# The head of a decay-attention and two-MLP kernel, put in order by a small list scheduler

## The chip, the cores and the metric

The kernel runs on one core of one Trainium2 chip. The metric is the device time of one execution in microseconds (us), lower is better. The profile is one execution of the same program, recorded by the hardware profiler; its times are counted from the start of its span. Engines: PE is the matrix engine (TensorE), DVE the vector engine, ACT the scalar engine, POOL is GpSimd, SP is the engine that issues most of the transfers.

## What is computed

Cut from the reference: a linear attention with a decay for each head, then two MLPs on its output.

```python
# q, k, v: batch 2, 8 heads, 768 steps, head size 64, float32
for t in range(S):
    state = gamma * state + einsum('bhd,bhe->bhde', k[:, :, t], v[:, :, t])
    y[:, :, t] = scale * einsum('bhd,bhde->bhe', q[:, :, t], state)
x = y.transpose(0, 2, 1, 3).reshape(1536, 512)
h = x @ w_in                                  # 512 -> 2048
g = where(h > 0, h, exp(minimum(h, 0)) - 1)
x = g @ w_out                                 # 2048 -> 512
out = ((x @ w_a) * (x @ w_b)) @ w_out2        # 512 -> 1536 -> 512
```

The weights arrive as 64-bit floats.

## The kernel before

**Attention.** The two batches times four pairs of heads make eight "pairs". A pair's 768 steps are six chunks of 128, worked in two halves of three chunks. Per pair, PE makes the chunk states (10 small matmuls into a bank `yk`, L271) from keys that ACT has scaled (`decay_k`, two instructions, `kd`, L232); DVE copies the first state and carries the decay through the others (`st`, L274 and L276). Per half, PE makes scores (6 matmuls into `sc`, L246), DVE masks them (`a`, L254), PE adds the state part and the score part of the result (10 or 12 matmuls into a bank `yk`, L294 and L300), DVE scales it (`yf`, L308), ACT rounds it to the high part `xh` (L320) and POOL makes the rest `xl` (L321).

**Products of the MLPs.** A number is held as a high and a low part, so each product is three matmuls (`mm3`, L384 to L386). Tokens come in three blocks of 512, features in groups of four tiles of 128. A "unit" is one group for one block. Its first layer (`l1_elu`) makes four feature tiles, each of 12 matmuls of 128x512 into `p`; for each, ACT takes relu and exp (`m`, L415 and L416), DVE combines (`r`, L418), ACT rounds (`gh`, L406) and POOL subtracts (`gl`, L408). Its second layer (`l2_elu`) makes four tiles `p` of 12 matmuls, each of which reads all four `g` tiles of the unit and all four weight tiles of `w2`. The second layer of a unit runs behind the first layer of the next one.

**Weights.** A conversion (`w_steps`) turns one 512 KB weight tile from 64-bit floats into a pair `wh`, `wl`: two ACT instructions on the raw words (L106, L107), four DVE instructions (L110, L113, L114, L117), one on ACT (`wh`, L122), one on POOL (`wl`, L124). The weight order begins with the four `w1` tiles (numbers 0 to 3) and the four `w2` tiles (4 to 7) of the first group. Number 8 is the next group's first.

**What sets the order.** Every engine works through its own list in order. The lists are written by the Python program: in the attention by hand, with `step` and `convert` calls that put pieces of conversions and the four feature tiles of the first unit between the pairs; in the MLPs by `tick`, which after every tile advances all running conversions by one piece and starts another at every second tick. `get` pushes a conversion on until its weight tile is there. All eight conversions of the first group are issued before the second unit begins.

Of the kernel before, what the change touches and what calls it, by code (L numbers as in the profile page):

```python
# [9 lines left out]
F32 = mybir.dt.float32  # L10
# [9 lines left out]
P = 128  # L20
C = 128
# [37 lines left out]

@with_exitstack  # L60
def tile_kernel(ctx: ExitStack, tc: tile.TileContext, qk, kv, w1, w2, wa, wb, wo, tab, out):
# [21 lines left out]
    src = {"w1": w1, "w2": w2, "wa": wa, "wb": wb, "wo": wo}  # L83
    W, raw = {}, {}
    state = {"loaded": 0, "split": 0, "read": 0, "freed": 0, "tick": 0, "quota": 0, "lag": 1, "room": NW // 2, "auto": False}
    NS = 3

    def w_load():
        j = state["loaded"]
        if j >= state["quota"] or j - state["read"] >= NS:  # L90
            return False
        key = order[j]
        t = stg.tile([P, 512, 2], I32, tag="raw", name="raw")
        nc.sync.dma_start(out=t.rearrange("p n w -> p (n w)"), in_=src[key[0]][:, key[1]].bitcast(I32))
        raw[key] = t
        state["loaded"] += 1
        return True
# [74 lines left out]
    def attention(side):  # L172
        with (
            tc.tile_pool(name="acst", bufs=1) as cst,
            tc.tile_pool(name="ald", bufs=3) as ld,
            tc.tile_pool(name="atmp", bufs=2) as tmp,
            tc.tile_pool(name="ps_s", bufs=2, space=bass.MemoryType.PSUM) as ps_s,
            tc.tile_pool(name="ps_y", bufs=2, space=bass.MemoryType.PSUM) as ps_y,
# [17 lines left out]
            L, KD, A, ST = {}, {}, {}, {}  # L196
            both = {"qk": qk, "kv": kv}

            def load(p, srcs, cuts=(0, NCH)):
                for n, src in srcs.items():  # L200

                    if p == NHP - 1 or (p, n) == (NPAIR - 1, "kv"):
                        pool, tag = (act, {"qk": "ah", "kv": "al"}[n]) if p < NHP else (accs[0], "acc")
                        t = pool.tile([P, NCC * TB], F32, tag=tag, name=n)
                        t = t[:, : 2 * S].rearrange("p (n s) -> p n s", n=2)
                    else:
                        t = ld.tile([P, 2, S], F32, tag=n, name=n)
                    if (p, n) == (0, "kv"):
                        nc.scalar.dma_start(out=t[:, 0], in_=src[p, :, 0])
                        nc.sync.dma_start(out=t[:, 1], in_=src[p, :, 1])  # L210
                        L[p, n] = t
                        continue
                    for c0, c1 in zip(cuts, cuts[1:]):
                        nc.sync.dma_start(out=t[:, :, c0 * C : c1 * C], in_=src[p, :, :, c0 * C : c1 * C])
                    L[p, n] = t

            def masks(hp):
                for h in range(2 * hp, 2 * hp + 2):
                    nc.scalar.mul(mask[:, h], causal, rise(h))

            rot = [0]

            def bank(p):
                rot[0] += 1
                pool = ps0 if p <= NHP and rot[0] % 2 else ps_y
                return pool.tile([P, 512], F32, tag="p" if pool is ps0 else "y", name="yk")

            def decay_k(p):
                hp, k_ = p % NHP, L[p, "kv"][:, 0]
                kd = tmp.tile([P, NCH, 2, D], F32, tag="kd", name="kd", bufs=2)  # L230
                for h in range(2):
                    nc.scalar.mul(  # L232
                        kd[:, :, h, :],
                        k_.rearrange("p (c h d) -> p c h d", c=NCH, h=2)[:, :, h, :],
                        gk(2 * hp + h),
                    )
                KD[p] = kd

            def scores(p, half):
                hp = p % NHP  # L240
                q_, k_ = L[p, "qk"][:, 0], L[p, "qk"][:, 1]
                sc = ps_s.tile([P, 2, 512], F32, tag="sc", name="sc")
                for c in range(3):
                    s0 = (half * 3 + c) * C
                    for h in range(2):
                        nc.tensor.matmul(  # L246
                            sc[:, h, c * C : (c + 1) * C],
                            k_[h * D : (h + 1) * D, s0 : s0 + C],
                            q_[h * D : (h + 1) * D, s0 : s0 + C],
                            start=True,  # L250
                            stop=True,
                        )
                a = tmp.tile([P, 2, 3, C], F32, tag="a", name="a", bufs=3)
                nc.vector.tensor_tensor(  # L254
                    out=a,
                    in0=sc[:, :, : 3 * C].rearrange("p h (c t) -> p h c t", c=3),
                    in1=mask[:, 2 * hp : 2 * hp + 2, None, :].to_broadcast([P, 2, 3, C]),
                    op=ALU.mult,
                )
                A[p, half] = a  # L260

            def states(p):
                hp = p % NHP
                v_ = L[p, "kv"][:, 1]
                kd = KD[p]
                s_ = tmp.tile([P, NCH - 1, D], F32, tag="st", name="st")
                s_ps = bank(p)[:, : (NCH - 1) * D].rearrange("p (c d) -> p c d", d=D)
                for c in range(NCH - 1):
                    for h in range(2):
                        r = slice(h * D, (h + 1) * D)  # L270
                        nc.tensor.matmul(  # L271
                            s_ps[r, c, :], kd[:, c, h, :], v_[:, c * P + h * D : c * P + (h + 1) * D], start=True, stop=True
                        )
                nc.vector.tensor_copy(s_[:, 0, :], s_ps[:, 0, :])  # L274
                for c in range(1, NCH - 1):
                    nc.vector.scalar_tensor_tensor(  # L276
                        out=s_[:, c, :],
                        in0=s_[:, c - 1, :],
                        scalar=gc(hp),
                        in1=s_ps[:, c, :],  # L280
                        op0=ALU.mult,
                        op1=ALU.add,
                    )
                ST[p] = s_

            def outputs(p, half):
                b, hp = divmod(p, NHP)
                q_, v_, s_, a = L[p, "qk"][:, 0], L[p, "kv"][:, 1], ST[p], A.pop((p, half))
                y = bank(p + 1)[:, : 3 * C].rearrange("p (c t) -> p c t", c=3)
                for i in range(3):  # L290
                    c = half * 3 + i
                    for h in range(2 if c else 0):
                        r = slice(h * D, (h + 1) * D)
                        nc.tensor.matmul(  # L294
                            y[r, i, :], s_[r, c - 1, :], q_[r, c * C : (c + 1) * C], start=(c in (1, 3)), stop=False
                        )
                for i in range(3):
                    c = half * 3 + i
                    for h in range(2):
                        nc.tensor.matmul(  # L300
                            y[h * D : (h + 1) * D, i, :],
                            v_[:, c * P + h * D : c * P + (h + 1) * D],
                            a[:, h, i, :],
                            start=False,
                            stop=(i == 2),
                        )
                yf = tmp.tile([P, 3 * C], F32, tag="yf", name="yf", bufs=2)
                nc.vector.tensor_tensor(  # L308
                    out=yf.rearrange("p (c t) -> p c t", c=3),
                    in0=y,  # L310
                    in1=gy[:, hp, None, :].to_broadcast([P, 3, C]),
                    op=ALU.mult,
                )
                t0, t1 = b * S + half * 3 * C, b * S + half * 3 * C + 3 * C
                while t0 < t1:
                    blk, o = divmod(t0, TB)
                    n = min(t1 - t0, TB - o)
                    i0 = t0 - (b * S + half * 3 * C)
                    hi, lo = (x[:, hp, o : o + n] for x in x_block(blk))
                    nc.scalar.copy(hi, yf[:, i0 : i0 + n])  # L320
                    nc.gpsimd.tensor_tensor(out=lo, in0=yf[:, i0 : i0 + n], in1=hi.bitcast(F32), op=ALU.subtract)  # L321
                    t0 += n
# [249 lines left out]
```

## Time and profile before

| | |
|---|---|
| median of 3 runs | 623.52 us (620.75 to 623.67) |
| the profiled execution | 622.01 us, of which the span is 620.1 us |
| PE busy | 609.6 us, 98% of the span, 3168 matmul records |
| DVE, ACT, POOL busy | 359.6, 283.1 and 255.9 us |
| HBM read and written | 48.57 MB and 3.15 MB |

The span is the time from the first to the last instruction; the remaining 1.9 us of the profiled execution lie around it. A busy PE is not PE at its peak, because the records of matmuls overlap; so the pace of matmuls is read from the starts of successive rows.

### The profile page before, as it was taken

What the parts mean: (1) busy time and instruction counts of PE and PEld (TensorE: products, weight loads), DVE (VectorE), ACT (ScalarE), POOL (GpSimd) and SP (SyncE); (2) the same over time, 40 slices, a digit from 0 to 9 for tenths busy, and PEclk for the clock granted to TensorE, in tenths of its full rate; (3) what the DMA queues carried; (4) which work ended last, traced back from release to release, by engine and by line L of the source; (5) the groups of instructions that cost most, each with busy time, mean ns of one, the idle gap of its engine ahead of it and who ended that gap; (6) DMA issues with size and microseconds to landing.
All of it is one profiled execution on the core that took longest, in us unless ns stands there. A gap on an engine that the chain in (4) does not pass through costs nothing.

```text
span 620.1 us, 8076 instructions
## 1 busy us (share of the span) xinstructions
PE 609.6 (98%) x3168; PEld 502.5 (81%) x3168; DVE 359.6 (58%) x490; ACT 283.1 (46%) x506; POOL 255.9 (41%) x192
## 2 busy tenths in 40 slices
PE   7998999999999999999999999999999999999997
PEld 5876788888888888888888888888888888888886
DVE  3999758787774378529881282766065677212122
ACT  3565577778554456536752253553242444120110
POOL 0455555456445236517773352435133334211110
PEclk9998999999999999999999999999999999999999
DMA  8964114333331033202230031233022130001002
GB/s 333 414 244 153 51 53 107 105 100 97 102 93 43 4 105 96 69 0 72 98 103 0 1 102 35 80 94 99 1 68 69 59 86 27 0 1 51 18 34 103
DMA packets 14838, 52.24 MB, mean 84 GB/s; under 512 B 1616, under 2 KB 2512, under 8 KB 14800
## 3 DMA queue, kind: packets, MB, share of 16 engines
q1 hardware_dynamic: 14368, 50.99, 25.5%
q10 hardware_dynamic: 432, 0.73, 0.3%
q8 instruction: 25, 0.41, 0.3%
q14 instruction: 13, 0.11, 0.1%
HBM read 48.57 MB, written 3.15 MB: 83 GB/s over the span
## 4 chain that ended last, share of the span: by engine, by line
PE 93%; DVE 3%; ACT 2%; DMA 1%; issue 1%; SPq 0%; DVEq 0%
PE p L384 30%; PE p L385 30%; PE p L386 30%; DMA qk<-in_qk 1%; PE sc L246 1%; PE yk L300 1%; PE yk L294 1%; PE yk L271 1%; ACT kd L232 0%; DVE st L276 0%; DVE u L117 0%; DVE a L113 0%; DVE yf L308 0%; DVE a L254 0%; ACT a L106 0%
## 5 line engine op out<-in xcount | busy, mean ns | idle before, releaser
L124 POOL TENSOR_TENSOR wl<-u,wh 128x512 fp32r<-128x512 f32 x68 | 98.8, 1453 | 53.2 <-ACT wh L122 52.3
L408 POOL TENSOR_TENSOR gl<-pr,gh 128x512 fp32r<-128x512 f32 x36 | 50.5, 1402 | 156.9 <-ACT gh L406 156.9
L384 PE MATMUL p<-yh,wh 128*128 128x512 f32 x288 | 112.0, 389 | 0.0
L385 PE MATMUL p<-yl,wh 128*128 128x512 f32 x288 | 112.0, 389 | 0.0
L386 PE MATMUL p<-yh,wl 128*128 128x512 f32 x288 | 112.0, 389 | 0.0
L408 POOL TENSOR_TENSOR gl<-r,gh 128x512 fp32r<-128x512 f32 x48 | 72.7, 1514 | 85.3 <-ACT gh L406 85.3
L472 DVE TENSOR_TENSOR pr<-p,sa 128x512 f32<-128x512 f32 x36 | 24.9, 691 | 111.1 <-PE p L386 111.1
L117 DVE CUSTOM_DVE_ANT_0 u<-u,c 128x1024 uint16<-128x1024 uint16 x68 | 84.3, 1240 | 2.8
L110 DVE TENSOR_SCALAR a<-a 128x512 f32<-128x512 f32 x68 | 69.8, 1027 | 16.9 <-ACT a L106 16.7
L384 PE MATMUL p<-xh,wh 128*128 128x512 f32 x192 | 75.5, 393 | 0.0
L385 PE MATMUL p<-xl,wh 128*128 128x512 f32 x192 | 74.8, 390 | 0.0
L386 PE MATMUL p<-xh,wl 128*128 128x512 f32 x192 | 74.7, 389 | 0.0
L384 PE MATMUL p<-gh,wh 128*128 128x512 f32 x192 | 74.7, 389 | 0.0
L385 PE MATMUL p<-gl,wh 128*128 128x512 f32 x192 | 74.7, 389 | 0.0
L386 PE MATMUL p<-gh,wl 128*128 128x512 f32 x192 | 74.7, 389 | 0.0
L406 ACT CAST gh<-pr 128x512 fp32r<-128x512 f32 x36 | 22.4, 621 | 101.9 <-DVE pr L472 101.9
L385 PEld LDWEIGHTS p<-yl,wh 128*128 128x128 f32 x288 | 54.1, 188 | 11.3
L386 PEld LDWEIGHTS p<-yh,wl 128*128 128x128 f32 x288 | 54.1, 188 | 11.2
L384 PEld LDWEIGHTS p<-yh,wh 128*128 128x128 f32 x288 | 54.1, 188 | 11.1
L418 DVE SCALAR_TENSOR_TENSOR r<-m,p 128x512 f32<-128x512 f32 x48 | 32.9, 686 | 45.7 <-ACT m L416 39.6
L122 ACT CAST wh<-u 128x512 fp32r<-128x512 f32 x68 | 41.9, 615 | 33.5 <-DVE u L117 33.5
L385 PE MATMUL p<-wl,gh 128*128 128x512 f32 (+1 forms) x148 | 56.7, 383 | 0.0
(50 smaller groups left out, 956.1 us busy)
## 6 DMA issues: line engine op xcount, KB each, us to landing
raw<-in_w SPq DMA_DIRECT2D x32, 512.0 KB, 3.6
raw<-in_wa SPq DMA_DIRECT2D x12, 512.0 KB, 3.6
raw<-in_wb SPq DMA_DIRECT2D x12, 512.0 KB, 3.8
raw<-in_wo SPq DMA_DIRECT2D x12, 512.0 KB, 3.7
qk<-in_qk SPq DMA_DIRECT2D x7, 768.0 KB, 8.1
kv<-in_kv SPq DMA_DIRECT2D x7, 768.0 KB, 9.2
out<-oacc SPq DMA_DIRECT2D x11, 256.0 KB, 2.0
qk<-in_qk SPq DMA_DIRECT2D x2, 384.0 KB, 4.9
```

The lines of the kernel that those rows point to most:

```text
L110: nc.vector.tensor_scalar(a, a, E_LO, E_HI, op0=ALU.max, op1=ALU.min)
L117: nc.vector.tensor_tensor(out=u, in0=u, in1=c, op=ALU.add)
L122: nc.scalar.copy(hi, t)
L124: nc.gpsimd.tensor_tensor(out=lo, in0=t, in1=hi.bitcast(F32), op=ALU.subtract)
L246: nc.tensor.matmul(sc[:, h, c * C : (c + 1) * C], k_[h * D : (h + 1) * D, s0 : s0 + C], q_[h * D : (h + 1) * D, s0 : s0 + C], start=True, ...
L384: nc.tensor.matmul(ps, lh, rh, start=first, stop=False)
L385: nc.tensor.matmul(ps, lh, rl, start=False, stop=False)
L386: nc.tensor.matmul(ps, ll, rh, start=False, stop=last)
L406: nc.scalar.copy(hi, t)
L408: nc.gpsimd.tensor_tensor(out=lo, in0=t, in1=hi.bitcast(F32), op=ALU.subtract)
L418: nc.vector.scalar_tensor_tensor(out=r, in0=m, scalar=-1.0, in1=ps, op0=ALU.add, op1=ALU.max)
L472: nc.vector.tensor_tensor(out=pr, in0=pb, in1=sa, op=ALU.mult)
```

## The change

The attention, the first six conversions (0 to 5) and the first layer of the first unit become operations of a `Plan`. Each has an engine, an estimated duration, a rank, the operations it waits for, and the buffers it takes. `Plan.run` walks through a modelled time: it takes the operation that can start first, gives way to one of lower rank on the same engine that can start within 0.25 us, and emits its instructions. So each engine's list is in the order of that walk. A PE operation is held back while its rank is more than 4 above the lowest rank left (ranks over 100, the feature tiles, are exempt). Conversions 6 and 7 are only loaded in the plan; `tick` starts them, at every tick until eight are started. A feature tile is emitted in two halves of six matmuls. The copy of the first state goes from DVE to ACT. All masks are made before the first `kd`, with the load of `gy` behind the first two pairs of masks.

```diff
+class Ring:
+    def free_at(self):
+        if len(self.homes) < self.bufs:
+            return 0.0
+        users = self.homes[-self.bufs]
+        return None if any(u.end is None for u in users) else max((u.end for u in users), default=0.0)
...
+class Plan:
+    AHEAD, FILL = 4, 100
+    LAG = {"Q": 1.6}
...
+    def ready(self, o):
+        t = 0.0
+        for a in o.after:
+            if a.end is None:
+                return None
+            t = max(t, a.end + self.LAG.get(a.engine, 0.2) * (a.engine != o.engine))
+        for rings in o.takes:
+            ts = [x for x in (r.free_at() for r in rings) if x is not None]
+            if not ts:
+                return None
+            t = max(t, min(ts) + 0.2)
+        return t
+
+    def run(self, begin):
+        clock, left = dict(begin), list(self.ops)
+        while left:
+            best = None
+            last = min((o.rank for o in left if o.engine == "PE"), default=0) + self.AHEAD
+            far = lambda o: o.engine == "PE" and last < o.rank < self.FILL
+            for o in left:
+                t = self.ready(o)
+                if t is None or far(o):
+                    continue
+                t = max(t, clock[o.engine])
+                key = (t, o.rank)
+                if best is None or key < best[0]:
+                    best = key, o
+            (t, _), o = best
+            for p in left:
+                if p.engine == o.engine and p.rank < o.rank and not far(p):
+                    tp = self.ready(p)
+                    if tp is not None and max(tp, clock[o.engine]) <= t + 0.25:
+                        o = p
...
+            o.emit(*picked)
...
-    state = {"loaded": 0, "split": 0, "read": 0, "freed": 0, "tick": 0, "quota": 0, "lag": 1, "room": NW // 2, "auto": False}
-    NS = 3
+    state = {"loaded": 0, "split": 0, "read": 0, "freed": 0, "tick": 0, "quota": 0, "lag": 0, "room": NW // 2}
+    NS, NPL = 3, 6
...
-        if state["auto"] and state["tick"] % every == 0:
+        if state["split"] < 2 * G or state["tick"] % every == 0:
             convert()
...
+            need = lambda j: 32.0 + 3.5 * j if j < G else 60.0 + 3.0 * (j - G)
...
+                o = op("Q", 1.3, n - 14, fetch, takes=[([ring["raw"]], raw_)])
+                if j >= NPL:
+                    raw[key] = j
+                    return
+                o = op("ACT", 1.3, n - 8, words, [o], [([ring["da"]], a_), ([ring["dc"]], c_)], [raw_])
...
-                nc.vector.tensor_copy(s_[:, 0, :], s_ps[:, 0, :])
+                    nc.scalar.copy(st[:, 0, :], T["s", p][:, 0, :])
...
+                o = op("ACT", 1.15, z - 3, lambda *_: decay(), [done["k", p], t1_], [([ring["kd"]], kd_)], [K])
+                o = op("PE", 0.75, z + 1, states, [o, done["v", p]], [([ry, r0], s_)], [kd_, K])
+                o = op("ACT", 0.3, z + 1.1, first, [o], [([ring["st"]], st_)], [s_])
+                done["st", p] = op("DVE", 1.25, z + 1.5, scan, [o], uses=[st_, s_])
...
+                plan.run({"Q": 2.2, "PE": 4.2, "DVE": 1.4, "ACT": 2.3, "POOL": 0.4})
...
+            state.update(loaded=NPL + NS, split=NPL, read=NPL)
...
-        side = units[0][0](*units[0][2:])
-        attention(side)
-        for _ in side:
-            pass
+        attention()
         moe()
```

How the lists change is shown at three places. The numbers behind the names tell buffers apart.

ACT in the attention, before, around the scaled keys of the last pair (`kd_711`): relu and exp of a feature tile, the end of one conversion (`wh`), the end of the feature tile (`gh`), the start of another conversion (`a`, `c`), then `kd`.

```order
L415 ACTIVATE m_694<-p_681 128x512
L416 ACTIVATE m_694<-m_694 128x512
L122 CAST wh_698<-u_665 128x512
L406 CAST gh_702<-r_695 128x512
L106 ACTIVATE a_707<-raw_505 128x512
L107 ACTIVATE c_708<-raw_505 128x512
L232 ACTIVATE kd_711<-kv_436,tb1_96 128x6x64 x2
```

ACT in the attention now, around the scaled keys of the last two pairs (`kd_581`, `kd_588`):

```order
L354 ACTIVATE a_545<-raw_439 128x512
L355 ACTIVATE c_546<-raw_439 128x512
L522 CAST xh_213<-yf_560 128x128
L522 CAST xh_268<-yf_560 128x256
L414 ACTIVATE kd_581<-kv_496,tb1_96 128x6x64 x2
L414 ACTIVATE kd_588<-kv_524,tb1_96 128x6x64 x2
```

Both `kd` now stand ahead of every piece of a feature tile and of the `wh` that they stood behind.

ACT at the end of the second unit's first layer now: its third and fourth feature tiles (`p_992`, `p_1020`), the start of conversion 8 (`a_1047`), and the `wh` of conversions 6 and 7 (`wh_1059`, `wh_1067`).

```order
L620 ACTIVATE m_1005<-p_992 128x512
L621 ACTIVATE m_1005<-m_1005 128x512
L611 CAST gh_1015<-r_1006 128x512
L620 ACTIVATE m_1033<-p_1020 128x512
L621 ACTIVATE m_1033<-m_1033 128x512
L611 CAST gh_1042<-r_1034 128x512
L196 ACTIVATE a_1047<-raw_869 128x512
L197 ACTIVATE c_1048<-raw_869 128x512
L212 CAST wh_1059<-u_982 128x512
L212 CAST wh_1067<-u_1012 128x512
```

Before, the last `wh` of the first group (conversion 7, `wh_935`) stood ahead of the second unit's first tile (`p_959`); `p_893` is the last tile of the first unit.

```order
L106 ACTIVATE a_870<-raw_669 128x512
L107 ACTIVATE c_871<-raw_669 128x512
L320 CAST xh_248<-yf_885 128x256
L320 CAST xh_601<-yf_885 128x128
L415 ACTIVATE m_906<-p_893 128x512
L416 ACTIVATE m_906<-m_906 128x512
L406 CAST gh_913<-r_907 128x512
L320 CAST xh_601<-yf_931 128x384
L122 CAST wh_935<-u_891 128x512
L415 ACTIVATE m_972<-p_959 128x512
```

The two rounding steps have moved from ahead of the second unit's first tile to behind its fourth.

PE now, the first tile of the first unit's second layer, right behind the second unit's first layer:

```order
L589 MATMUL p_1052<-gh_737,wh_851 128x512
L590 MATMUL p_1052<-gl_738,wh_851 128x512
L591 MATMUL p_1052<-gh_737,wl_852 128x512
L589 MATMUL p_1052<-gh_882,wh_879 128x512
L590 MATMUL p_1052<-gl_883,wh_879 128x512
L591 MATMUL p_1052<-gh_882,wl_880 128x512
L589 MATMUL p_1052<-gh_905,wh_1059 128x512
L590 MATMUL p_1052<-gl_906,wh_1059 128x512
L591 MATMUL p_1052<-gh_905,wl_1060 128x512
L589 MATMUL p_1052<-gh_914,wh_1067 128x512
L590 MATMUL p_1052<-gl_915,wh_1067 128x512
L591 MATMUL p_1052<-gh_914,wl_1068 128x512
```

Its seventh matmul reads `wh` of conversion 6 and its twelfth `wl` of conversion 7.

## Rows read from the trace of the kernel before

**Rows 1.** Busy time by stretch: PE, weight loads, DVE, ACT, POOL, clock, DMA.

```profile
0.00:18.20 18.20, 14.79 (x136) 11.48 (x138) 7.24 (x16) 7.12 (x15) 0.24 (x5) 1.00 0.89 346
18.20:34.80 16.60, 16.47 (x268) 13.61 (x264) 15.97 (x35) 10.66 (x24) 9.35 (x11) 1.00 1.02 413
34.80:60.00 25.20, 21.39 (x234) 16.79 (x235) 22.80 (x39) 14.19 (x29) 12.73 (x13) 0.93 0.49 164
83.50:620.10 536.60, 533.41 (x2365) 442.14 (x2363) 298.76 (x379) 237.56 (x414) 219.39 (x151) 1.00 0.21 62
```

**Rows 2.** Timeline of PE, 0 to 100 us: start, duration, what, idle before.

```profile
14.87 1.05 PE L271 MATMUL yk<-kv,kd 128*64 128x64 f32 x20
...
18.23 0.75 PE L271 MATMUL yk<-kv,kd 128*64 128x64 f32 x20
...
23.55 1.17 PE L271 MATMUL yk<-kv,kd 128*64 128x64 f32 x20
```

**Rows 3.** Timeline of PE, 0 to 100 us: the two longest waits for ACT.

```profile
44.39 0.33 PE L271 MATMUL yk<-kv,kd 128*64 128x64 f32 x2 [0.52 <-ACT kd L232]
...
56.10 0.33 PE L271 MATMUL yk<-kv,kd 128*64 128x64 f32 x2 [2.73 <-ACT kd L232]
```

**Rows 4.** Busy time by stretch around 56 us, columns as in the first group.

```profile
50.00:56.00 6.00, 3.37 (x50) 2.65 (x48) 5.09 (x8) 3.56 (x8) 2.74 (x3) 1.00 0.38 127
56.00:60.00 4.00, 3.72 (x34) 3.21 (x35) 3.91 (x5) 1.35 (x5) 2.17 (x3) 0.57 0.17 19
```

**Rows 5.** Timeline of ACT around the second of these waits.

```profile
53.21 0.62 ACT L122 CAST wh<-u 128x512 fp32r<-128x512 f32 x1 [2.41 <-DVE u L117]
...
55.45 1.10 ACT L232 ACTIVATE kd<-kv,tb 128x384 f32<-128x384 f32 x2
```

**Rows 6.** Groups of DVE instructions from 4.7 to 83.5 us: count, busy, mean ns, idle.

```profile
L254 DVE TENSOR_TENSOR a<-sc,mask 128x768 f32<-128x768 f32 x16 | 15.2, 951 | 7.7 <-PE sc L246 7.7
L276 DVE SCALAR_TENSOR_TENSOR st<-st,tb,yk 128x64 f32<-128x64 f32 x32 | 9.0, 281 | 1.1
L308 DVE TENSOR_TENSOR yf<-yk,gy 128x384 f32<-128x384 f32 x16 | 8.7, 549 | 1.6 <-PE yk L300 1.5
L113 DVE TENSOR_SCALAR a<-a 128x512 int32<-128x512 int32 x8 | 7.6, 945 | 0.2
L114 DVE SCALAR_TENSOR_TENSOR u<-raw,a 128x512 int32<-128x512 int32 x8 | 6.6, 830 | 0.4
L117 DVE CUSTOM_DVE_ANT_0 u<-u,c 128x1024 uint16<-128x1024 uint16 x8 | 6.2, 772 | 0.0
L110 DVE TENSOR_SCALAR a<-a 128x512 f32<-128x512 f32 x8 | 5.2, 651 | 3.1 <-ACT a L106 3.1
```

**Rows 7.** Timeline of ACT in the second unit's first layer.

```profile
79.93 0.62 ACT L406 CAST gh<-r 128x512 fp32r<-128x512 f32 x1 [0.81 <-DVE r L418]
80.46 0.59 ACT L415 ACTIVATE m<-p 128x512 f32<-128x512 f32 x1
...
82.47 0.62 ACT L406 CAST gh<-r 128x512 fp32r<-128x512 f32 x1 [0.75 <-DVE r L418]
...
84.11 0.58 ACT L415 ACTIVATE m<-p 128x512 f32<-128x512 f32 x1
```

**Rows 8.** Timeline of all engines, 91 to 93.5 us: a conversion's last steps.

```profile
91.37 0.63 ACT L122 CAST wh<-u 128x512 fp32r<-128x512 f32 x1
...
92.08 1.33 POOL L124 TENSOR_TENSOR wl<-u,wh 128x512 fp32r<-128x512 f32 x1 [1.29 <-ACT wh L122]
...
92.40 1.57 DVE L117 CUSTOM_DVE_ANT_0 u<-u,c 128x1024 uint16<-128x1024 uint16 x1
```

**Rows 9.** Timeline of PE, 0 to 100 us: the second unit's first layer and what follows.

```profile
75.31 0.39 PE L384 MATMUL p<-xh,wh 128*128 128x512 f32 x1
...
83.25 0.39 PE L386 MATMUL p<-xh,wl 128*128 128x512 f32 x1
83.48 0.39 PE L384 MATMUL p<-gh,wh 128*128 128x512 f32 x1
```

More of the change, by code (lines that the diff above doesn't have):

```diff
@@ new lines, with __init__, op @@
+class Plan:
+    AHEAD, FILL = 4, 100
+    LAG = {"Q": 1.6}
+    def __init__(self):
+        self.ops = []
+    def op(self, engine, cost, rank, emit, after=(), takes=(), uses=()):
+        o = Op(engine, cost, rank, emit, [a for a in after if a], [t[0] for t in takes], [t[1] for t in takes])
+        for users in [*o.users, *uses]:
+            users.append(o)
+        self.ops.append(o)
+        return o
+    def ready(self, o):
[30 more added lines that the diff above has]
+                        o = p
+            t = max(t, self.ready(o))
+            picked = []
+            for rings, users in zip(o.takes, o.users):
+                ring = min((r for r in rings if r.free_at() is not None), key=lambda r: r.free_at())
+                ring.homes.append(users)
+                picked.append(ring)
+            o.end = t + o.cost
+            clock[o.engine] = o.end
+            left.remove(o)
+            o.emit(*picked)
+        return clock
@@ L195, in attention @@
                 nc.tensor.matmul(warm[:, 0, : 3 * C], zero[:, :C], zero, start=True, stop=True)
[L196 to L235, printed above, removed]
-                    )
-                KD[p] = kd
@@ L239, in scores @@
[L239 to L244, printed above, removed]
-                    for h in range(2):
[L246 to L251, printed above, removed]
-                        )
[L253 to L260, printed above, removed]
@@ L286, in outputs @@
[L286 to L322, printed above, removed]
@@ new lines, in attention, with tile_of, home @@
+            plan = Plan()
+            op = plan.op
+            ring = {n: Ring(k) for n, k in dict(qk=3, kv=3, kd=2, a=3, st=2, yf=2, raw=3, da=2, dc=2, du=2, m=3, r=3).items()}
+            rsc, ry, r0 = Ring(2), Ring(2), Ring(2)
+            rsc.homes.append([])
+            T, done = {}, {}
+            def tile_of(key, p_, shape, tag, dt=F32):
+                T[key] = p_.tile(shape, dt, tag=tag, name=tag)
+                return T[key]
+            def home(p, n):
+                if p == NHP - 1:
+                    t = act.tile([P, NCC * TB], F32, tag={"qk": "ah", "kv": "al"}[n], name=n)
+                elif (p, n) == (NPAIR - 1, "kv"):
+                    t = accs[0].tile([P, NCC * TB], F32, tag="acc", name=n)
+                else:
+                    return tile_of((n, p), ld, [P, 2, S], n)
+                T[n, p] = t[:, : 2 * S].rearrange("p (n s) -> p n s", n=2)
+                return T[n, p]
@@ new lines, in attention, with load, emit @@
+            users = {}
+            src = {"qk": qk, "kv": kv}
+            def load(p, n, cost, rank, cut=slice(None), col=slice(None), eng=None):
+                first = (n, p) not in users
+                inst = users.setdefault((n, p), [])
+                own = p == NHP - 1 or (p, n) == (NPAIR - 1, "kv")
+                def emit(*_):
+                    t = home(p, n) if first else T[n, p]
+                    (eng or nc.sync).dma_start(out=t[:, cut, col], in_=src[n][p, :, cut, col])
+                takes = [([ring[n]], inst)] if first and not own else ()
+                return op("Q", cost, rank, emit, takes=takes, uses=() if takes else [inst])
@@ new lines, in part, with high, low @@
+            def part(p, blk, key, o, yf_, cols, from_, rank):
+                hp, n = p % NHP, cols.stop - cols.start
+                def high():
+                    nc.scalar.copy(x_block(blk)[0][:, hp, cols], T["yf", key][:, from_])
+                def low():
+                    hi, lo = (x[:, hp, cols] for x in x_block(blk))
+                    nc.gpsimd.tensor_tensor(out=lo, in0=T["yf", key][:, from_], in1=hi.bitcast(F32), op=ALU.subtract)
+                o = op("ACT", 0.2 + n / 1280, rank, high, [o, blk == NB - 1 and done["y", (NHP - 1, 1)]], uses=[yf_])
+                done["x", blk, key] = op("POOL", 0.25 + n / 500, rank, low, [o], uses=[yf_])
@@ L382, in mm3 @@
+            with pool(name="atA", bufs=3) as atA:
+                for p in range(NPAIR):
+                    pair(p)
+                for j in range(NPL + NS):
+                    weight(j)
+                for f in range(G):
+                    tile_f(f, 4 * f)
+                plan.run({"Q": 2.2, "PE": 4.2, "DVE": 1.4, "ACT": 2.3, "POOL": 0.4})
+            raw.update({k: T["raw", j] for k, j in raw.items()})
+            state.update(loaded=NPL + NS, split=NPL, read=NPL)
     def mm3(ps, lhs, rhs, first, last):
```

283 lines of the change are left out of this document (199 added, 84 removed).

## The prediction

> **What bounds the kernel now.** I read the busy time by stretch first. From 83.5 us to the end PE is busy 533.4 of 536.6 us at a granted clock of 1.00 [rows 1]: the second layer of the first unit begins at 83.48 us, and from there on one matmul follows another every 0.227 us (36 of them from 75.31 to 83.48 us [rows 9]). The change leaves that part's matmuls as they are, so 536.6 us stay, and the question is when PE gets there, and whether it then has what it needs.
>
> The head is the part to judge. In the timeline of PE, a pair of the attention costs 5.32 us where nothing waits (states to states, 18.23 to 23.55 us [rows 2]). Between 34.8 and 60 us PE is busy only 21.4 of 25.2 us [rows 1]. The timeline shows the holes: PE waits for `kd` from ACT, 0.52 us at 44.39 and 2.73 us at 56.10 us [rows 3]. ACT was not slow there; its list was badly ordered: `kd` of the last pair starts at 55.45 us, behind a `wh` that itself sat 2.41 us waiting for DVE [rows 5]. Behind the long hole the granted clock is 0.57 over 56 to 60 us [rows 4], which by the two levels is mostly 1.2 GHz in place of 2.4: 4.0 us at 0.57 lose 1.7 us of PE's work. DVE is the other limit: it is busy 15.97 of 16.60 us from 18.2 to 34.8 us and 22.80 of 25.2 after that [rows 1]. Transfers are near their limit up to 34.8 us (share 1.02) and at half of it after [rows 1]. The plan asks for the same bytes in nearly the same order, so I cost them at nothing; a late load would move a pair by about its own duration.
>
> **What the change gives back.** Both waits for `kd` go, since `kd` of the last pairs now stands ahead of the `wh` and of the feature tiles. Moreover three of the four feature tiles of the first unit and the ends of conversions 4 and 5 move behind the attention, and conversions 6 and 7 leave the head. When does the attention end? Two sums bound it.
>
> By PE: at 18.23 us the old list has issued the scores and states of pairs 0 and 1 and the results of pair 0; the new list has the same set done there. Left are six pairs (6 x 5.32 = 31.9), the results of pair 1 (22 of a pair's 44 matmuls, an estimate of 2.9), and the one feature tile that still stands inside (12 x 0.227 = 2.7): 18.23 + 37.5 = 55.7 us, if PE never waits.
>
> By DVE: up to its last `yf` it has 16 `a`, 32 steps of `st` and 16 `yf` (15.2 + 9.0 + 8.7 us), four whole conversions at 0.651 + 0.945 + 0.830 + 0.772 = 3.20 us and three instructions of a fifth (2.4) [rows 6], and one `r`, for which ACT waits 0.75 us [rows 7]: 48.9 us. To this come the 11.0 us that it is idle before 18.2 us (18.20 - 7.24 [rows 1]): 59.9 us. The records of successive instructions overlap somewhat, so that is the upper end. The copy that goes to ACT is left out of this sum. On ACT no row shows that copy; the nearest is a rounding of 128x512 at 0.63 us [rows 8], an upper bound, and the lower one is nothing; eight of them fit the 5.9 us that ACT is idle from 18.2 to 34.8 us [rows 1].
>
> I take 58.5 us, nearer DVE's sum, because DVE and not PE is the saturated engine where conversions run. Then come three tiles of the first unit and four of the second, 7 x 12 x 0.227 = 19.1 us, and 0.2 for the change of shape (an estimate, one matmul's pace). So PE would reach the second layer of the first unit at T = 77.8 us, where it was 83.48: **5.7 us gained**, with bounds of 4.3 and 8.5 from the two sums.
>
> **What it costs.** At T PE needs all four `w2` tiles. Before, conversion 7's `wh` was issued before the second unit. Now `wh` of 6 and 7 stand on ACT behind everything of the second unit's four tiles and behind the start of conversion 8, and ACT waits in order. The walk, with T as origin: the first of these tiles ends at T - 8.17 + 0.16 (a last matmul starts at 83.25, takes 0.39, and the next tile starts at 83.48 [rows 9]), so its relu starts at T - 8.0. From one relu to the next ACT needs 3.65 us where the two raw-word instructions of a conversion stand between (80.46 to 84.11) and 2.54 us where none does (2.01 from relu to `gh`, 0.53 from `gh` to relu [rows 7]). The first two tiles carry conversions 6 and 7, the third none: the fourth tile's relu starts at T - 8.0 + 3.65 + 3.65 + 2.54 = T + 1.8, though PE finished that tile at T + 0.2. Its `gh` starts 2.01 later, and behind it, with conversion 8's two instructions between, `wh` of 6 starts after another 1.64 (82.47 to 84.11 [rows 7]): T + 5.5. POOL's `wl` starts 0.71 after its `wh` (91.37 to 92.08) and takes 1.33 [rows 8]; two of them one after the other end at T + 5.5 + 0.7 + 2.7 = T + 8.9. The twelfth matmul of the first tile should start at T + 11 x 0.227 = T + 2.5. **Loss 6.4 us** if ACT and DVE come to it without a backlog. They don't quite: the ends of conversions 4 and 5 stand on DVE ahead of the first unit's `r`, and conversion 6's addition and 7's shift and joining ahead of the last `r`. I add 1.0 for both, 7.4 in all. Bounds: 4.7 if ACT kept pace with PE (the 1.7 us of backlog gone), 9.2 if both delays cost an instruction that waits for POOL (1.33 [rows 8]) or a little more.
>
> On DVE a total that is 0.77 us on average took 1.57 when it was issued at 92.40 us, while POOL worked from 92.08 to 93.41; it ended 0.56 after POOL did [rows 6, 8]. The Trainium skill (SBUF — State Buffer, section "SBUF: two separate sides") says that DVE and GpSimd share one pair of ports as an exclusive lock, held for a whole instruction. The trace agrees, with 1.57 us for that addition. By that rule each of the DVE steps named would stand still for the rest of a POOL subtraction, and the sum would be about 628 us; by the mean row it is what I take.
>
> Behind a hole of some 4 us, with smaller ones after it, I expect PE's clock to fall as it did behind the 2.73 us one, where 1.7 us were lost [rows 3, 4]. I take 1.5, since part of the slow time falls into the remaining waits. The bounds are nothing, if the clock is back before the last wait ends, and 2.5, if the broken stretch holds it down longer.
>
> After that the list is short of nothing: conversion 8 starts two ticks later than before, but its weights are needed only with the next group, some 30 us on, and PE is busy without a hole there now [rows 1].
>
> **Sum.** 620.1 - 5.7 + 7.4 + 1.5 = 623.3 us of span, and 1.9 around it: 625.2 us, against 622.0 for the profiled execution. That execution is 1.5 under the median of the three runs (623.5), within their spread; I leave the number on its base.
>
> **The rivals.**
> *Not slower: PE sets the attention's pace.* With POOL's and DVE's work spread out, DVE's conversions run shorter than their means (0.945 for the shift contains waits for POOL) and the attention ends at PE's 55.7 us. Price 2.8 us: 622.4 us. For it speaks that PE does without a hole 5.32 us a pair with one conversion per pair [rows 2]; against it that DVE had only 0.6 us left in that stretch [rows 1]. The gain is as large as the cost once the attention ends at 55.3 us.
> *The hole is short.* ACT has no backlog and the clock holds: 620.1 - 5.7 + 4.7 + 1.9 = 621.0 us. Against it: the 3.65 us per tile with a conversion are longer than PE's 2.72 [rows 7, 9], twice in a row. Together with the first rival, 618.2 us.
> *DVE waits for POOL at each place named*, in the ends of conversions 4 and 5 and ahead of the last `r`: 1.33 us three times, of which 1.0 is in my sum: 628 us. For it speaks the 1.57 us row [rows 8]; against it that POOL has gaps between its subtractions.
>
> **How the numbers follow.** Forecast as summed, 625.2 us: 0.40. PE's pace 0.20; the short hole 0.12, both of these together 0.08; DVE behind POOL 0.20. The two ends of the range are 620.5 and 630: below lies mostly the case of both rivals together, above a late attention (59.9 us) with the long hole and the slow clock. A measurement of this kernel can tell about 0.5% (3.1 us) from no change. The forecast is 3.2 us above before, on that edge, so its weight is shared between same and slower; the first two rivals count as same, both together as faster, DVE behind POOL as slower. With a little for what I don't see: faster 0.11, same 0.44, slower 0.45.
>
> **What would show it.** In the new profile: no wait of PE for `kd` past 35 us; the last small matmul (`yk`) at 57 to 60 us; the first `p` from `gh` at 76 to 80 us; then, in that tile, a wait of PE for `wh` of some 4 us and for `wl` twice, and a granted clock under 1 there; PE dense from the next tile on for 534 us. I am wrong if `wh` of conversion 6 is there when PE comes, if PE still waits in the attention for DVE by more than 3 us in sum, or if holes appear past 100 us.

## The result, and the profile after

The changed kernel takes 628.18 us (median of 5 runs, 626.79 to 630.49), the kernel before, run beside it, 621.63 (5 runs, 620.61 to 623.67). The ratio is 1.0101, with a 95% interval of 1.008 to 1.0122: 1% slower. The profiled execution took 629.84 us, its span is 628.0.

The busy time by stretch of the changed kernel (columns as in [rows 1]):

```profile
18.20:34.80 16.60, 16.60 (x276) 14.12 (x276) 14.65 (x27) 10.28 (x24) 6.92 (x9) 1.00 1.02 412
34.80:60.00 25.20, 22.45 (x274) 17.43 (x272) 21.26 (x40) 13.28 (x31) 12.76 (x15) 0.86 0.39 138
60.00:80.00 20.00, 19.18 (x115) 15.34 (x112) 11.77 (x16) 12.22 (x22) 11.70 (x10) 1.00 0.19 53
80.00:100.00 20.00, 14.06 (x54) 10.58 (x53) 12.93 (x18) 10.62 (x20) 8.13 (x6) 0.83 0.27 79
```

From 18.2 to 34.8 us PE now has no hole at all, where it had 0.13 us. But from 34.8 to 60 us it is busy 22.45 of 25.2 us at a granted clock of 0.86, where it had been 21.39 at 0.93 [rows 1]. And there is a hole of 6 us behind 80 us, where PE had been dense.

The timeline of PE shows where it waits (start, duration, what, idle before and releaser):

```profile
18.21 0.94 PE L463 MATMUL sc<-qk 64*128 64x128 f32 x12
...
37.95 0.94 PE L463 MATMUL sc<-qk 64*128 64x128 f32 x12 [0.74 <-DVE a L469]
...
41.00 0.33 PE L421 MATMUL yk<-kv,kd 128*64 128x64 f32 x2 [0.49 <-ACT kd L414]
41.50 0.80 PE L421 MATMUL yk<-kv,kd 128*64 128x64 f32 x18 [0.18 <-ACT kd L414]
43.64 1.65 PE L463 MATMUL sc<-qk 64*128 64x128 f32 x12 [1.34 <-DVE a L469]
...
62.76 0.50 PE L589 MATMUL p<-xh,wh 128*128 128x512 f32 x1
...
69.34 0.50 PE L589 MATMUL p<-xh,wh 128*128 128x512 f32 x1 [0.82 <-DVE r L555]
...
83.08 0.39 PE L589 MATMUL p<-gh,wh 128*128 128x512 f32 x1
...
84.21 0.39 PE L591 MATMUL p<-gh,wl 128*128 128x512 f32 x1
90.15 0.79 PE L589 MATMUL p<-gh,wh 128*128 128x512 f32 x1 [5.56 <-ACT wh L212]
90.74 0.63 PE L590 MATMUL p<-gl,wh 128*128 128x512 f32 x1
91.75 0.79 PE L591 MATMUL p<-gh,wl 128*128 128x512 f32 x1 [0.38 <-POOL wl L214]
...
93.20 0.63 PE L591 MATMUL p<-gh,wl 128*128 128x512 f32 x1
93.62 0.63 PE L589 MATMUL p<-gh,wh 128*128 128x512 f32 x1
```

The longer wait for `kd` of [rows 3] is gone; the 0.52 us one has a successor of 0.49 at 41.0 us. In their place stand waits for masks (`a`, 0.74 and 1.34 us). The attention ends at 62.76 us, and PE reaches the second layer at T = 83.08 us, 0.4 before the 83.48 of [rows 9]. So the head gave back almost nothing. Then six matmuls run and the seventh waits 5.56 us for `wh` of conversion 6. The second tile should start 12 x 0.227 us after T, at 85.8, and starts at 93.62: 7.8 us lost. From there to the end are 534.4 us, 0.5 more than before (536.6 less the first tile's 2.7), since two more matmuls run at the low clock. In all -0.4 + 7.8 + 0.5 = 7.9 us, the difference of the spans (628.0 - 620.1).

The granted clock around both places, by stretch:

```profile
43.50:46.00 2.50, 2.36 (x14) 2.04 (x15) 2.36 (x8) 1.86 (x5) 2.50 (x3) 0.50 0.91 357
46.00:48.00 2.00, 2.00 (x6) 1.13 (x4) 1.91 (x4) 0.00 (x0) 0.01 (x1) 0.50 0.43 178
48.00:50.00 2.00, 2.00 (x17) 1.60 (x18) 1.87 (x3) 1.03 (x2) 0.73 (x1) 0.50 0.88 240
50.00:52.00 2.00, 2.00 (x16) 1.27 (x12) 1.34 (x5) 0.00 (x0) 1.51 (x2) 0.99 0.06 23
...
90.00:92.00 2.00, 1.46 (x3) 0.74 (x4) 0.80 (x3) 0.62 (x2) 1.82 (x2) 0.50 0.11 43
92.00:94.00 2.00, 2.00 (x5) 1.46 (x6) 1.97 (x2) 0.14 (x1) 0.93 (x1) 0.50 0.00 0
94.00:96.00 2.00, 2.00 (x9) 1.60 (x8) 0.21 (x1) 0.97 (x2) 0.95 (x1) 0.89 0.67 178
```

After the waits of 37 to 43.6 us PE runs at 1.2 GHz (0.50) for the 6.5 us from 43.5 to 50; that loses 3.2 us of its work. Behind the hole it is slow for some 4 us (90.15 to 94.3), and a part of that hides behind POOL's `wl`.

The hole is the length of ACT's list, and of POOL's two `wl` behind it. The timeline of ACT shows it (relu, `gh`, raw words, `wh`):

```profile
75.11 0.60 ACT L620 ACTIVATE m<-p 128x512 f32<-128x512 f32 x1
...
78.84 0.59 ACT L620 ACTIVATE m<-p 128x512 f32<-128x512 f32 x1
...
82.59 0.57 ACT L620 ACTIVATE m<-p 128x512 f32<-128x512 f32 x1
...
85.17 0.59 ACT L620 ACTIVATE m<-p 128x512 f32<-128x512 f32 x1
...
87.86 0.62 ACT L611 CAST gh<-r 128x512 fp32r<-128x512 f32 x1 [1.43 <-DVE r L623]
88.38 0.66 ACT L196 ACTIVATE a<-raw 128x512 f32<-128x512 f32 x1
88.95 0.64 ACT L197 ACTIVATE c<-raw 128x512 int32<-128x512 uint32 x1
89.50 1.12 ACT L212 CAST wh<-u 128x512 fp32r<-128x512 f32 x2
```

From relu to relu it takes 3.73, 3.75 and 2.58 us; PE's tiles take 2.72. So the fourth relu starts 2.1 us after T, its `gh` waits 1.43 us for DVE, and `wh` of conversion 6 starts at T + 6.4. The timelines of DVE and POOL show what that `gh` waited for, and the two `wl`:

```profile
85.35 1.33 POOL L613 TENSOR_TENSOR gl<-r,gh 128x512 fp32r<-128x512 f32 x1 [2.24 <-ACT gh L611]
85.59 1.64 DVE L204 SCALAR_TENSOR_TENSOR u<-raw,a 128x512 int32<-128x512 int32 x1
87.15 0.68 DVE L623 SCALAR_TENSOR_TENSOR r<-m,p 128x512 f32<-128x512 f32 x1
...
90.18 2.76 POOL L214 TENSOR_TENSOR wl<-u,wh 128x512 fp32r<-128x512 f32 x2 [0.35 <-ACT wh L212]
```

The joining of conversion 7 (L204) took 1.64 us while POOL worked, where conversion 6's took 0.69 at 81.26 us, and `r` stood behind it.

### The profile page after: what moved, and what is told of

Its sections match the earlier page's. It is cut to its first block, busy times and chain, and to the rows that moved or that the text cites. A ratio compares the mean times of both kernels' runs of the same rounds, so it can differ in the third digit from the quotient of the medians.

```text
span 628.0 us, 8080 instructions
## 1 busy us (share of the span) xinstructions
PE 612.6 (98%) x3168; PEld 503.9 (80%) x3168; DVE 359.5 (57%) x482; ACT 285.3 (45%) x514; POOL 255.4 (41%) x192
## 3 DMA queue, kind: packets, MB, share of 16 engines
q1 hardware_dynamic: 14368, 50.99, 25.2%
## 4 chain that ended last, share of the span: by engine, by line
PE 89%; DVE 2%; ACT 1%; issue 1%; POOL 0%; DVEq 0%
PE p L589 29%; PE p L591 29%; PE p L590 29%; PE yk L490 1%; PE sc L463 1%; PE yk L484 1%; DVE u L367 1%; DVE r L623 0%; ACT m L621 0%; ACT gh L611 0%; DVE a L363 0%; ACT a L196 0%; ACT c L197 0%; ACT m L620 0%; POOL wl L214 0%
## 5 line engine op out<-in xcount | busy, mean ns | idle before, releaser
L214 POOL TENSOR_TENSOR wl<-u,wh 128x512 fp32r<-128x512 f32 x62 | 90.5, 1460 | 48.4 <-ACT wh L212 47.4
L613 POOL TENSOR_TENSOR gl<-r,gh 128x512 fp32r<-128x512 f32 x44 | 68.3, 1552 | 90.3 <-ACT gh L611 78.8
L207 DVE CUSTOM_DVE_ANT_0 u<-u,c 128x1024 uint16<-128x1024 uint16 x62 | 79.3, 1279 | 2.7
L200 DVE TENSOR_SCALAR a<-a 128x512 f32<-128x512 f32 x62 | 66.3, 1069 | 21.1 <-ACT a L196 21.0
L591 PE MATMUL p<-wh,gl 128*128 128x512 f32 (+1 forms) x148 | 56.7, 383 | 0.0
L589 PE MATMUL p<-wh,gh 128*128 128x512 f32 (+1 forms) x148 | 56.7, 383 | 0.0
```

The lines of the kernel that those rows point to most:

```text
L200: nc.vector.tensor_scalar(a, a, E_LO, E_HI, op0=ALU.max, op1=ALU.min)
L207: nc.vector.tensor_tensor(out=u, in0=u, in1=c, op=ALU.add)
L214: nc.gpsimd.tensor_tensor(out=lo, in0=t, in1=hi.bitcast(F32), op=ALU.subtract)
L589: nc.tensor.matmul(ps, lh, rh, start=first, stop=False)
L591: nc.tensor.matmul(ps, ll, rh, start=False, stop=last)
L613: nc.gpsimd.tensor_tensor(out=lo, in0=t, in1=hi.bitcast(F32), op=ALU.subtract)
```

## The experiments

Two questions: is the hole made by the two late conversions, and why is the attention late? My theory for the second, from the trace, is that conversion steps stand ahead of masks on DVE and are held up there by POOL; rivals are the order alone, the copy on ACT, and the feature tile inside the attention. Ratios are to the kernel before, on the same chip, with 95% intervals. "T" is the start of the first unit's second layer in the profile. Executions of one kernel differ by 1 to 7 us, in part by the first 15 us (last section), so places in the trace decide where totals are close. Differences to the changed kernel are between medians of separate measurements, in which the kernel before had 621.6 to 622.5 us.

**Conversions 6 and 7 ahead of the second unit.**

```diff
         attention()
+        while state["split"] < 2 * G or running:
+            if state["split"] < 2 * G:
+                convert()
+            else:
+                advance()
         moe()
```

> The changed kernel, with conversions 6 and 7 issued whole between the first unit and the second. Theory (the hole at the first second-layer tile comes from the two late conversions, and costs 8.2 us): the 5.56 us wait for wh is gone, the time falls by 8 us to about 620 us, and the attention still ends near 62.8 us. Rival (ACT's backlog is the cause and only moves): ACT now stands still for some 5 us behind the two conversions, the second unit's tiles wait for it, and the time falls by less than 4 us, to 624 or more.

619.25 us (618.57 to 620.27), ratio 0.9959 (0.9945 to 0.9974). The timeline of PE in this run, at the matmuls of the second layer's first tile that follow one another on three weight tiles `wh`:

```profile
81.36 0.39 PE L589 MATMUL p<-gh,wh 128*128 128x512 f32 x1
...
82.04 0.39 PE L589 MATMUL p<-gh,wh 128*128 128x512 f32 x1
...
82.72 0.39 PE L589 MATMUL p<-gh,wh 128*128 128x512 f32 x1
```

They follow at the dense pace; no matmul waits there. The time falls by 8.9 us, the 8.3 of the hole and its slow clock, and a little of the attention's scatter. The rival falls: ACT did stand still for the conversions (2.77 us ahead of the two `wh`), and PE did not wait for it.

**All eight conversions in the plan** (`NS, NPL = 3, 8` in place of `3, 6`).

> The changed kernel, with all eight conversions in the plan. Theory: the hole is gone as in the run with 6 and 7 ahead of the second unit, and since the plan puts 6 and 7 behind the attention's last pairs anyway, the attention ends where it did: about 620 us. Rival (two conversions more on DVE push the attention back, which was why they were left out): the attention ends 2 to 4 us later, 622 to 624 us.

619.87 us (619.01 to 622.83), ratio 0.9978 (0.9963 to 0.9993). No hole, and the attention ends at 61.6 us, not later. So the theory holds and the rival falls. The waits for masks stay (1.73 and 1.34 us); what comes late is one `r` behind the conversions, for which PE waits 1.63 us at 69.0.

**The old kernel with the two conversions late**, the one part of the change alone.

```diff
         j = state["split"]
+        if not state["auto"] and j >= 6:
+            return
...
-        if state["auto"] and state["tick"] % every == 0:
+        if state["auto"] and (state["split"] < 2 * G or state["tick"] % every == 0):
```

> The kernel before, with only one part of the change: no more than six conversions in the attention, 6 and 7 by the ticks of the second unit. Theory: the same hole as in the changed kernel opens at the first second-layer tile, 5 to 6 us of wait and a half clock behind it, 6 to 8 us in all, less up to 2 us that the shorter list gives back in the attention: 626 to 630 us. Rival (the hole is made by the plan's order in the attention): no hole, 620 to 622 us.

630.25 us (629.9 to 631.37), ratio 1.0138 (1.0123 to 1.0153). The timeline of PE in this run, behind the same six matmuls:

```profile
89.12 0.79 PE L386 MATMUL p<-gh,wh 128*128 128x512 f32 x1 [5.50 <-ACT wh L122]
...
90.72 0.79 PE L388 MATMUL p<-gh,wl 128*128 128x512 f32 x1 [0.37 <-POOL wl L124]
```

That is the hole again, to 0.06 us, without any plan. The time is 0.25 us above the theory's range.

**Conversion 8 two ticks later.**

```diff
-        if state["split"] < 2 * G or state["tick"] % every == 0:
+        if state["split"] < 2 * G or (state["tick"] > 4 and state["tick"] % every == 0):
```

> The changed kernel, with conversion 8 started at the sixth tick in place of the fourth, so that its two ACT instructions (1.1 us) no longer stand ahead of the two late wh. Theory (the hole is the length of ACT's list ahead of these wh): PE's wait for wh shrinks by 1.1 us, from 5.6 to 4.4 to 4.6, the wait for wl stays or grows by under 0.3, and the time falls by about 1 us, to 626.5 to 627.5. Rival (DVE or POOL sets the hole's end): the hole keeps its length, 628 us.

The timeline of PE in this run, at the same hole:

```profile
89.28 0.55 PE L589 MATMUL p<-gh,wh 128*128 128x512 f32 x1 [4.45 <-ACT wh L212]
89.63 0.63 PE L590 MATMUL p<-gl,wh 128*128 128x512 f32 x1
91.34 0.80 PE L591 MATMUL p<-gh,wl 128*128 128x512 f32 x1 [1.08 <-POOL wl L214]
```

The wait for `wh` shrinks by 1.11 us, as ACT's list does; the wait for `wl` grows by 0.70, more than expected, for POOL becomes the next in line. The total, 628.85 us (627.91 to 630.59; 1.0114, 1.0086 to 1.0143), missed the range that I expected, and can't show the 0.4 that is left: in this profile the second score product alone waited 2.61 us for its data, against 0.36 in the changed kernel's.

**Conversions ranked 12 us later**, masks ahead of them (`need`: `44.0 + ...` and `72.0 + ...` in place of `32.0` and `60.0`).

> The changed kernel, with all conversions ranked 12 us later, so that masks and results of the attention come ahead of them on DVE; the hole at the second layer stays. Theory (PE's waits for masks, and the half clock from 43.5 to 50.4 us that follows them, come from conversion steps that stand ahead of masks on DVE and there wait for POOL): both go, the attention ends near 57 to 58 us in place of 62.8 (the first tile of the unit still inside); the conversions are late by a part of that at the first unit's tiles, so the time falls by 2 to 5 us, to 623 to 626. Rival (the copy on ACT or the feature tile inside the attention causes the waits): they stay, 627 to 629 us.

The busy time by stretch of this run (columns as in [rows 1]):

```profile
34.80:60.00 25.20, 23.27 (x316) 18.83 (x312) 24.03 (x43) 14.41 (x34) 13.16 (x16) 1.00 0.49 165
```

The waits for masks from 37 to 44 us are gone, the clock is 1.00 there, and the attention ends at 57.2 us, as the theory says; one wait for a mask is left ahead of the last result (1.21 us at 56.4). But T is 80.61 only, 2.5 us earlier: the conversions now stand on DVE ahead of the first unit's `r`, where PE waits 1.94 us at 65.3, and from 60 to 80 us the clock is 0.91 (1.00 in the changed kernel). And the total, 628.53 us (627.9 to 629.11; 1.011, 1.0094 to 1.0127), missed my range and is no less than the changed kernel's. So more than half of what the attention gained was lost again at the tiles behind it, and the rest, read from this run's fastest execution (627.90 us), doesn't show in the median.

**The copy of the first state back on DVE** (`nc.vector.tensor_copy`, and in the plan an operation of DVE of 0.25).

> The changed kernel, with the copy of the first state back on DVE, in the plan too. Theory (waits for masks come from conversion steps ahead of them on DVE): the waits for masks stay or grow a little, the hole stays, 627 to 630 us. Rival (the hop over ACT delays the states and so the results): the attention ends 1 to 3 us earlier, 625 to 627 us.

627.15 us (626.01 to 628.46), ratio 1.0078 (1.0047 to 1.0109). PE waits 0.90 and 0.96 us for masks and 0.68 for `kd`: they stay, so the hop over ACT is not what makes them. The median is 1.0 us below the changed kernel's, inside both intervals. In this profile the clock stayed at 1.00 after nearly the same waits, and T is 80.03, 3.1 us earlier: the 3.2 us that the changed kernel lost at the low clock are as large as that, and a share of the copy in it is not shown.

**All feature tiles behind the attention** (each waits for the last result).

> The changed kernel, with all four feature tiles of the first unit behind the last result of the attention. Theory: the waits for masks at 37.9 and 43.6 us stand ahead of the tile and stay (2 us); what follows them, the half clock up to 50 us, now meets small matmuls instead of the tile, so the time is the same within 1.5 us, 627 to 630 us. Rival (the tile inside holds PE or a bank and causes the late attention): the attention ends more than 4 us earlier (its own 2.7 us and the wait), and the time falls by 1.5 us or more, to under 626.7.

629.74 us (629.44 to 630.9), ratio 1.0129 (1.0104 to 1.0154). PE waits 0.47 and 1.34 us for masks and 0.68 for `kd`, as before; the last result ends 4.3 us earlier, 2.7 of which is the tile, and T falls by 1.3 only. The rival asked for such an end, but for a shorter time too, which did not come. The clock from 34.8 to 60 us is 0.93 in place of 0.86 here, which is worth about that much. So the tile is not what makes the masks late.

**POOL without the weights' low parts.** In the plan, `wl` is filled by a transfer of `wh` from ACT's queue; the subtraction is left out, so the weights' low parts are not those of the kernel. DVE's list is the same.

```diff
-                    nc.gpsimd.tensor_tensor(out=lo, in0=T["du", j].bitcast(F32), in1=hi.bitcast(F32), op=ALU.subtract)
+                    nc.scalar.dma_start(out=lo.bitcast(F32), in_=hi.bitcast(F32))
```

> The changed kernel, in which POOL leaves out the subtraction that makes the low part of the six planned weight tiles (a transfer issued by ACT fills them with the high part instead; the list of DVE is unchanged). Theory (conversion steps on DVE are long where they meet POOL, by about 3 us from 32 to 42 us, and the masks behind them are late by that): those steps come nearer to their short durations (0.4 to 0.7 us; POOL's work on x stays and can still be met), PE's wait for masks of 2.1 us and its wait for kd of 0.7 us shrink by half or more, the attention ends 2 to 5 us earlier (the higher figure if the half clock goes too), the hole stays: 624 to 627 us. Rival (the order of the list alone makes the masks late): the waits for masks stay at about 2 us, 627 to 629 us.

623.31 us (622.67 to 624.84), ratio 1.0016 (1.0006 to 1.0027): 4.9 us less than the changed kernel, and 0.7 under the range expected. The busy time by stretch of this run (columns as in [rows 1]):

```profile
34.80:60.00 25.20, 25.20 (x346) 20.06 (x343) 23.64 (x48) 16.39 (x38) 12.54 (x15) 1.00 0.58 217
```

And its timeline of DVE, two conversion steps and the mask behind them:

```profile
38.03 0.70 DVE L359 TENSOR_SCALAR a<-a 128x512 f32<-128x512 f32 x1
...
39.56 0.69 DVE L367 SCALAR_TENSOR_TENSOR u<-raw,a 128x512 int32<-128x512 int32 x1
...
41.04 0.94 DVE L469 TENSOR_TENSOR a<-sc,mask 128x768 f32<-128x768 f32 x1
```

The same steps in the changed kernel's timeline of DVE:

```profile
37.82 1.50 DVE L359 TENSOR_SCALAR a<-a 128x512 f32<-128x512 f32 x1
...
40.62 1.27 DVE L367 SCALAR_TENSOR_TENSOR u<-raw,a 128x512 int32<-128x512 int32 x1 [0.50 <-issue]
...
42.63 0.95 DVE L469 TENSOR_TENSOR a<-sc,mask 128x768 f32<-128x768 f32 x1
```

And the changed kernel's timeline of POOL at that time:

```profile
37.76 1.28 POOL L384 TENSOR_TENSOR wl<-u,wh 128x512 fp32r<-128x512 f32 x1 [1.28 <-ACT wh L380]
40.20 1.14 POOL L526 TENSOR_TENSOR xl<-yf,xh 128x128 fp32r<-128x128 f32 x2 [1.16 <-ACT xh L522]
```

The list alone makes no mask late: PE waits for nothing from 12 us to the hole, the clock stays at 1.00 from 18 us to the hole, and T is 77.86. From the clamp to the next mask DVE needs 3.0 us in place of 4.8. The timeline of PE in this run, at a score product at the point of the list that the changed kernel reaches at 18.21 us, at the first tile behind the attention, and at T:

```profile
20.01 0.94 PE L463 MATMUL sc<-qk 64*128 64x128 f32 x12
...
58.56 0.50 PE L589 MATMUL p<-xh,wh 128*128 128x512 f32 x1
...
77.86 0.39 PE L589 MATMUL p<-gh,wh 128*128 128x512 f32 x1
```

From there to the attention's end PE needs 38.55 us, and 44.55 in the changed kernel (18.21 to 62.76): the 6.0 between them are the 2.75 us of waits and the 3.2 lost at the low clock. This run started 1.8 us late, which could hide waits. But the run with conversion 8 later has the same list up to there and the same late start (20.03 us at this point), and its timeline of PE has the waits:

```profile
39.57 0.94 PE L463 MATMUL sc<-qk 64*128 64x128 f32 x12 [0.53 <-DVE a L469]
...
45.24 1.65 PE L463 MATMUL sc<-qk 64*128 64x128 f32 x12 [1.33 <-DVE a L469]
```

Its T is 83.31, 5.5 us behind. This decides between POOL and the order alone.

**Both repairs, and more.** Eight conversions in the plan, ranked 12 us later:

> Both repairs together: all eight conversions in the plan, and all ranked 12 us later. If the two add up: the hole goes (8 us) and the attention ends near 57 us, of which the first unit's tiles give back half, so about 617 us. If DVE then has the conversions to do behind the attention, where the tiles' r wait for them: PE waits 3 to 5 us for r there and the time is 619 to 621 us, no better than with eight conversions at the old ranks.

617.99 us (616.19 to 620.5), ratio 0.9941 (0.9922 to 0.996), between the two forecasts (617 and 619 to 621), and 1.9 us less than with eight conversions at the old ranks; PE waits 2.3 us for `r` and 1.7 for masks. The same with the copy on DVE:

> All eight conversions in the plan, ranked 12 us later, with the copy of the first state on DVE. If the copy on ACT costs something once masks are first (PE waited 0.7 us for it in the run without this change): 0.5 to 1.5 us less than that run, 616.5 to 617.5 us. Else the same within 0.5 us, or more, since DVE gets 2 us of work: 618 to 619 us.

616.88 us (616.03 to 618.17), ratio 0.991 (0.989 to 0.993), the fastest kernel of this study, 0.9% under the kernel before. T is 76.42, and the first tile there waits under 1 us in sum. That is in the range forecast for a copy that costs something on ACT, but its gain of 1.1 us over the run ahead of it lies inside the intervals. And 6 and 7 ahead of the second unit, the others ranked 8 us later:

> Conversions 6 and 7 whole between the first and the second unit, and the six planned ones ranked 8 us later. The hole is gone and the attention shorter than with the old ranks by 2 to 3 us, a part of it given back at the first unit's tiles: 617 to 619 us, near the run with eight planned ones at ranks 12 later. If the two late conversions now come too late for the earlier second layer, PE waits there again by 1 to 3 us: 619 to 621 us.

620.78 us (617.64 to 624.42), ratio 0.9968 (0.9948 to 0.9988): no wait at the second layer, but three for masks (2.6 us in sum) and 2.43 for an `r`. That is 1.8 us above the range, and no better than with the old ranks (619.25). The 619 to 621 us of the other case are met, but not by its wait.

## Why the prediction was right or wrong

*The hole: right, in place, cause and size.* The forecast had the first `wh` at T + 5.5, or 6.5 with the 1.0 for delays on DVE, and the twelfth matmul 7.4 us late; `wh` started at T + 6.4, and the twelfth matmul (93.20) 7.6 us late. The last `wl` ended at T + 9.9 (92.94 us), where the forecast had 8.9 and the 1.0. The backlog of ACT is as worked out (3.7, 3.7, 2.6 us per tile). The old kernel with that one edit gets the same wait; without the late conversions it is gone.

*The clock behind the hole: a little too dear.* 1.5 us were set; the last three matmuls of the first tile and the first two of the next lost about 0.2 us each, some 1 us. The first two of these ran while POOL still made the last `wl`, so about 0.6 us is the clock's own. Hole and clock together cost 8.3 us (7.8 + 0.5), against 8.9.

*The gain in the head: the step that failed.* "I take 58.5 us", from PE's sum of 55.7 and DVE's of 59.9; it was 62.8, outside both. Of PE's two waits for `kd` the long one did go, and the sum of DVE's work was about right (a conversion's four steps averaged 3.16 us against 3.20). But a sum for each engine is a lower bound on when both are done, not an upper one: it has no term for the waits of one for the other. PE waited 2.75 us (0.74 + 0.49 + 0.18 + 1.34), then lost 3.2 at the low clock, and 0.8 more for an `r` among the tiles. PE's sum itself was 1.0 too short: without a wait its list took 38.55 us where the sum has 37.5. The low clock behind short waits had no term in the head. That T is 77.86 in the run without POOL's subtractions, against 77.8, is luck: that run started 1.8 us late, so with the changed kernel's start it would be at about 76.1 (an estimate from these rows). There PE's pace bounds the attention, not DVE's sum. Of the signs, the wait for `kd`, the last small matmul (62.8 us) and T failed; the limit of 3 us of waits for DVE was not reached (2.1 us).

*"DVE behind POOL" was a rival with the right mechanism, but not at all its places.* I put it at the conversions' ends and ahead of the last `r`, and gave it 0.20. Ahead of the last `r` it came (the 1.64 us above), within the 1.0 set for it; it also struck in the middle of the attention, where the plan puts conversion steps just ahead of masks. In the changed kernel the clamp issued at 37.82 us takes 1.50 us and ends 0.28 after POOL's subtraction of 37.76 to 39.04. The Trainium skill (SBUF — State Buffer, section "SBUF: two separate sides") says that GpSimd and a DVE operation that takes the shared ports exclude each other: whichever starts first has them for the whole instruction, and the other blocks. The trace agrees. The plan's costs (0.5, 0.6, 0.9 and 0.8 us) know nothing of it.

*The rivals "PE sets the pace" and "the hole is short"* are refuted by the waits above. The total, 628.2 us, lies inside the range, at its upper part: the hole came as forecast, and the head gave 0.4 us in place of 5.7. That it lies there is luck in part. The profiled execution is 4.6 us above the forecast and the median 1.7 us below that execution; and the 628 us of "DVE waits for POOL" fit although its 3 us were to come at the hole, where they did not.

What stays open: how much of the attention's lateness is the clock's own scatter. Over 43.5 to 50 us it was 0.50 in the changed kernel's profile, 0.74 to 0.76 in four runs with much the same waits (all eight conversions in the plan, 6 and 7 ahead, conversion 8 later, feature tiles behind) and 1.00 with the copy on DVE. The five executions of the changed kernel had mean clocks of 0.988 to 0.995, and the fastest (626.79 us) had the highest.

## What to carry to other kernels

When work is moved behind a stage to shorten it, find its first consumer and walk the in-order list of each engine between: here two conversions cost 8 us because their last steps stood behind four tiles of another unit on ACT. Sums of busy time per engine bound a stage from below; a list made from fixed durations needs slack, or a rule (none was tried here), where two engines hold each other up. Mending the first needs one number (eight conversions in the plan, 8 us). Giving the tight chain a priority brought another 2 together with that, and nothing in the two other runs that tried it.

## What the hardware showed beyond expectation

Three waits of PE of 0.7 to 1.3 us stood ahead of 6.5 us at 1.2 GHz in the profiled execution (waits at 37.2, 40.5 and 42.3 us, granted clock 0.50 from 43.5 to 50 us); with the copy on DVE nearly the same waits (0.90, 0.68, 0.96 us) were followed by no fall. I had reckoned with a fall only behind a hole of several us.

The first 15 us are not the same from execution to execution: the second score product waited 0.36 us for its data in the changed kernel's profile, 2.61 in that of the run with conversion 8 later and 2.79 in that of the run without POOL's subtractions, with the same transfers issued ahead of it.
